# The third pair's q is turned right behind the first run of u, in a linear attention and gated layer kernel

## The chip, the cores and the metric

The kernel runs on one core of a Trainium2 chip. The metric is the time on the device in microseconds (us). Before the change it was 1086.03 us, the median of three runs (1085.31 to 1089.51). The profiled execution, from which all views of the kernel before are taken, has a span of 1088.1 us from its first to its last instruction.

In the text, TensorE (PE in the profile) is the matrix engine, VectorE (DVE) and ScalarE (ACT) are the engines for elementwise work, GpSimd (POOL) forms differences of weights, and SyncE (SP) issues nearly all transfers. Loading the stationary operand of a matmul is an instruction of its own and has its own row, PEld.

## What is computed

Attention without a softmax, an RMS norm per head, and then a gated feed-forward layer:

```python
# q, k, v: batch 8, heads 8, sequence 576, head size 64, all float32
kv = np.einsum('bhsd,bhse->bhde', k, v)
out = np.einsum('bhsd,bhde->bhse', q, kv)          # u in the kernel
rms = np.sqrt(np.mean(out * out, axis=-1, keepdims=True) + 1e-06)
attn = out / rms * g_norm

# x: 4608 tokens of 512 (all heads of one place side by side)
gate = 1.0 / (1.0 + np.exp(-(x @ w_gate)))          # 512 -> 1536
val = x @ w_val                                     # 512 -> 1536
y = gate * val @ w_out                              # 1536 -> 512
```

The three weight matrices are stored as doubles, and the kernel converts them to float32 itself at its start.

## The kernel before

**Two streams of work.** The 4608 tokens are cut into nine chunks of 512 (`G`). The feed-forward layer goes over chunks 0 to 8, and the attention over batches 0 to 7 of 576 tokens. Batches 0 and 1 are computed at the start by an order of tokens written out by hand, together with chunk 0 and the conversion of the weights. From then on, while chunk c (1 to 6) is in the feed-forward layer, the attention of batch c + 1 (2 to 7) is woven into it. This is the part that the change touches; the text calls batches 3 to 7 *later batches*. Chunks 7 and 8 have no attention beside them.

**A chunk of the feed-forward layer.** The chunk is computed by a Strassen-like scheme with seven products in place of eight. The first layer (`first_layer_fast`, line 682) has six blocks. In each, seven steps are taken for two columns of blocks in turn: one product for the first, one for the second (line 692, four matmuls in the source and eight records in the trace), followed by the VectorE or ScalarE instruction that takes the result out of the accumulator bank: a copy (L700), sigmoids (L710, L724), additions (L706, L714, L719, L723, L728). At the end of a block come the two multiplications by the gate (L731) and four sums for the second layer (L761 to L764), all on VectorE. The second layer (`second_layer_fast`, line 766) has 14 products of six matmuls each (line 778); its evacuations are L785 to L808.

**Slots.** The attention of the next batch is a queue of small steps, `fill`. Each call of `slot()` takes one step from the queue and emits it at that place of the program. The first layer calls it after each of the seven steps of a block, so 42 times in a chunk; the second layer calls it after every third matmul, so 28 times. Thus a step's place in the queue is its place in every engine's order of work. [...]`spread` puts the queue together: in the first layer, a step on VectorE is only given slots 2 to 5 of a block (1 to 5 in chunk 1), and empty steps are put in ahead of it until such a slot comes.

**The steps of a batch** come from `feed(b)` (line 341), which handles the four pairs of heads of the batch:

- `turn(n, e)` (line 366): q of pair n, head e, is turned from rows to columns by a VectorE transpose (L369), 96 partitions x 384. There are two turns per pair. The turned q goes to `qTs`, which has room for two pairs (pair n uses half n % 2). Behind the second turn of pair n, `load_q(n + 1)` asks for the q of the next pair (L100, 288 KB). The tile for q has one buffer, so this transfer waits for the second turn to have read it.
- `kv_mm` (L353, L359): k times v of all four pairs on TensorE, and `kv_copies` (L364), eight copies to `kvq` on VectorE.
- `two_pairs(n0)` (line 374), called for the first two pairs and for the last two. It returns nine steps: `u_mm` (L393, 72 small matmuls in the source and 144 records, the first pair's half and then the second's), the square on ScalarE (L399), two sums on VectorE (L402), the root on ScalarE (L405, with a load of another activation table ahead of it), a reciprocal and two norms on VectorE (L409, L411), and two steps that turn the result back (L418, two transposes each) and send it by DMA into the next chunk's x (L428).

At the end of the queue, the sums over the next chunk's x are put in (`x_sums`, L669 to L672), which need those transfers. The accumulator tile of u has one buffer (tag `at`), which `u_mm` of the last two pairs takes over from the first two.

**The order around the change**, in slots of the chunk from 0, for a later batch: turns of the first pair 2 and 3; kv matmuls 8; copies 9 to 19; turns of the second pair 23 and 24; u of the first two pairs 25; square 26; sums 30 and 31; root 32; norms 33 and 37; x turns 38 and 39; turns of the third pair 40 and 42; turns of the fourth pair 44 and 45; u of the last two pairs 46 and the other steps behind it, the last x turn at 54; sums over x asked for at 59. Slot 42 is the first of the second layer.

Of the kernel before, what the change touches and what calls it, by code (L numbers as in the profile page):

```python
# [20 lines left out]
def kernel(  # L21
# [223 lines left out]
    def chunk(c):  # L245
        if c not in xT:
            xT[c] = sb.tile([P, NMT, G], FP32, tag="xT", name="xT", bufs=3)
        return xT[c]
# [90 lines left out]
    PE, DVE, ACT = range(3)  # L339

    def feed(b):

        early = b == 2
        d = {}

        def kv_mm():
            mains, rest = kv_late[b]
            d["kv"] = ps = at_ps()
            for n in range(NHP):
                for j in range(NK4):  # L350
                    for e in range(2):
                        c = slice(NK4 * HD * e + HD * j, NK4 * HD * e + HD * j + HD)
                        nc.tensor.matmul(ps[HD * e:HD * e + HD, n, 0:HD], mains[n, "k"][:, c], mains[n, "v"][:, c],  # L353
                                         start=(j == 0), stop=False)
            for i in range(NHP // 2):
                for r in range(2):
                    for e in range(2):
                        n, rs, c = NHP // 2 * r + i, slice(PH * r, PH * r + PH), HD * (2 * i + e)
                        nc.tensor.matmul(ps[HD * e:HD * e + HD, n, 0:HD], rest[rs, c:c + HD],  # L359
                                         rest[rs, GH + c:GH + c + HD], start=False, stop=True)  # L360

        def kv_copies(i, rs):
            for r in rs:
                nc.vector.tensor_copy(out=kvq[QB * r:QB * r + QB, :, i], in_=d["kv"][QB * i:QB * i + QB, :, 0:HD])  # L364

        def turn(n, e):

            w_ = NJ * HD
            nc.vector.transpose(qTs[0:NP, n % 2, w_ * e:w_ * e + w_],  # L369
                                pairs[n]["q"][:, e].rearrange("p (j i c) -> p i j c", i=NC, c=QB))  # L370
            if e == 1:
                load_q(n + 1)

        def two_pairs(n0):


            d = {}
            ms = sb.tile([P, NQ, NJ], FP32, tag="ms2", name="ms2", bufs=1)
            sq = sqs[:, 0:2 * S].rearrange("p (r c) -> p r c", r=NQ)
            units = [slice(NJ // 2 * i, NJ // 2 * (i + 1)) for i in range(2)]  # L380

            def by_head(t):
                return t.rearrange("p r (n d) -> p r n d", d=HD)

            def u_mm():
                d["u"] = u = at_ps()[:, 0:NQ, 0:2 * QC]
                for which in range(2):
                    for g in range(JH):
                        for i in range(NC):
                            for r in range(NQ):  # L390
                                for e in range(2):
                                    c, o = NJ * HD * e + QC * i + PH * g, HD * (JH * which + g)
                                    nc.tensor.matmul(u[HD * e:HD * e + HD, r, o:o + HD],  # L393
                                                     qTs[QB * r:QB * r + QB, (n0 + which) % 2, c:c + PH],
                                                     kvq[QB * r:QB * r + QB, (n0 + which) % NHP, NC * e + i],
                                                     start=(i == 0), stop=(i == NC - 1))

            def u_square():
                nc.scalar.activation(out=sq, in_=d["u"], func=AF.Square)  # L399

            def u_sum(i):
                nc.vector.tensor_reduce(out=ms[:, :, units[i]], in_=by_head(sq)[:, :, units[i]], axis=AX.X, op=ALU.add)  # L402

            def u_root():
                nc.scalar.activation(out=ms, in_=ms, func=AF.Sqrt, bias=eps, scale=1.0 / HD)  # L405

            def u_norm(i):
                if i == 0:
                    nc.vector.reciprocal(ms, ms)  # L409
                m_ = ms[:, :, units[i]]  # L410
                nc.vector.tensor_tensor(out=by_head(sq)[:, :, units[i]], in0=by_head(d["u"])[:, :, units[i]],  # L411
                                        in1=m_.unsqueeze(3).to_broadcast([P, NQ, NJ // 2, HD]), op=ALU.mult)

            def x_turn(i):


                for which in range(2):
                    nc.vector.transpose(xTs[:, i, which],  # L418
                                        sq.rearrange("p r (w g i c) -> p w i r g c", w=2, g=JH, i=NC)[:, which, i])
                m = n0 % NHP  # L420
                for j in range(2):
                    for e in range(2):
                        p0, p1 = HD * e + QB * j, HD * e + QB * i
                        s0 = 0
                        while s0 < S // 2:
                            c, o = divmod(S * b + S // 2 * j + s0, G)
                            n_ = min(G - o, S // 2 - s0)
                            nc.sync.dma_start(out=chunk(c)[p1:p1 + QB, m:m + 2, o:o + n_],  # L428
                                              in_=xTs[p0:p0 + QB, i, :, s0:s0 + n_])
                            s0 += n_  # L430

            return ([(PE, u_mm), (ACT, u_square), (DVE, lambda: u_sum(0)), (DVE, lambda: u_sum(1)), (ACT, u_root),
                     (DVE, lambda: u_norm(0)), (DVE, lambda: u_norm(1))] +
                    [(DVE, lambda i=i: x_turn(i)) for i in range(NC)])

        def turns_of(n):
            return [(DVE, lambda n=n, e=e: turn(n, e)) for e in range(2)]

        n0 = NHP * b
        steps = turns_of(n0)  # L440

        if b > 2:
            steps += [(PE, idle)] * 4
        steps.append((PE, kv_mm))
        for i in range(2 * NC):
            for rs in ((0, 1), (2,)):
                steps.append((DVE, lambda i=i, rs=rs: kv_copies(i, rs)))
        steps += turns_of(n0 + 1) + two_pairs(n0) + turns_of(n0 + 2) + [(PE, idle)] + turns_of(n0 + 3)
        return steps + two_pairs(n0 + 2) + [(PE, idle)] * 4

    def idle():
        pass
# [61 lines left out]
    def at_ps():  # L514
        return psum.tile([P, 4, 512], FP32, tag="at", name="at")
# [35 lines left out]
    def plain(c, f, ps):  # L551

        blk = Plain(c, f, ps)
        for at in range(2 * NMT):
            blk.mm(*divmod(at, NMT))
            if at in (0, 2) and late:
# [8 lines left out]
    steps = {"KV": KV, "KVO": KV_OUT, "Q": Q, "QO": Q_OUT, "U": U, "SQ": U_SQUARE, "SUM": U_SUM, "ROOT": U_ROOT,  # L565
             "NORM": U_NORM, "X": X, "XO": X_OUT}
# [283 lines left out]
    for c in range(1, NG):  # L850
        if c + 1 < B:
            steps = feed(c + 1)
            if c == 1:

                i = 4
                while w2_sums:
                    steps.insert(i, (DVE, w2_sums.popleft()))
                    i += 3
            spread(steps, (1, 2, 3, 4, 5) if c == 1 else (2, 3, 4, 5))
        first_layer_fast(c)  # L860
        sums_of(c + 1)
        second_layer_fast(c)
        flush()
# [30 lines left out]
```

## Time and profile before

| | before |
|---|---|
| time, median of 3 | 1086.03 us (1085.31 to 1089.51) |
| span of the profiled execution | 1088.1 us, mean granted TensorE clock 0.994 |
| TensorE matmul / weight load busy | 1074.0 us (99%) / 888.0 us (82%) |
| VectorE / ScalarE / GpSimd busy | 637.7 us (59%) / 242.6 us (22%) / 291.3 us (27%) |
| L393, weight loads of u | 1728, busy 21.6 us, 9.5 us idle ahead of them |
| L369, turns of q | 48, busy 26.4 us, 17.3 us idle ahead of them, waiting for q |
| L669, first sum over x | 8, busy 5.5 us, 13.7 us idle ahead of them, waiting for x |

How to read the profile: the page gives busy time per engine and the chain of work that ended last. A list of groups gives, per line and operation, the busy time, the mean time of one, and how long its engine sat idle just before it and what ended that. The chain of waits says who waited for whom, with the total in us, the number of times and the longest. The order of time (timeline) has one line for instructions of a kind that follow each other, with the start, the time to the last one's end, the engine and line, the operation, what is written and read, and their number; in square brackets stands an idle time before it and what ended it. "issue" is time in which the engine waited for nothing that the profile shows. Busy times of matmuls are modelled at their ends; the starts of the weight loads are the firmer measure of when TensorE goes on.

The chunks can be told apart by the first weight load of L692 in each: chunk 2 runs from 275.17 us, chunk 3 from 393.78, chunk 4 from 510.44, chunk 5 from 628.97, chunk 6 from 745.49, chunk 7 from 862.17 and chunk 8 from 970.95.

### The profile page before, as it was taken

What the parts mean: (1) busy time and instruction counts of PE and PEld (TensorE: products, weight loads), DVE (VectorE), ACT (ScalarE), POOL (GpSimd) and SP (SyncE); (2) the same over time, 40 slices, a digit from 0 to 9 for tenths busy, and PEclk for the clock granted to TensorE, in tenths of its full rate; (3) what the DMA queues carried; (4) which work ended last, traced back from release to release, by engine and by line L of the source; (5) the groups of instructions that cost most, each with busy time, mean ns of one, the idle gap of its engine ahead of it and who ended that gap; (6) DMA issues with size and microseconds to landing.
All of it is one profiled execution on the core that took longest, in us unless ns stands there. A gap on an engine that the chain in (4) does not pass through costs nothing.

```text
span 1088.1 us, 18239 instructions
## 1 busy us (share of the span) xinstructions
PE 1074.0 (99%) x7226; PEld 888.0 (82%) x7226; DVE 637.7 (59%) x1261; ACT 242.6 (22%) x473; POOL 291.3 (27%) x390
## 2 busy tenths in 40 slices
PE   9999999999999999999999999999999999999997
PEld 8544448888888888888888888888888888888886
DVE  4897747784477447662767347744766266516631
ACT  4654321221113111311122111311131112001200
POOL 0000024440254024420444025402442055205500
PEclk9999999999999999999999999999999999999998
DMA  9944710012400140013201130024001200010001
GB/s 255 251 155 155 241 39 12 12 25 62 118 12 11 51 130 12 13 45 78 81 12 40 47 118 12 11 57 137 1 12 37 56 3 1 1 37 3 1 1 39
DMA packets 69108, 64.89 MB, mean 60 GB/s; under 512 B 23712, under 2 KB 63008, under 8 KB 69024
## 3 DMA queue, kind: packets, MB, share of 16 engines
q1 hardware_dynamic: 68768, 63.69, 21.1%
q8 instruction: 58, 0.95, 0.4%
q14 instruction: 26, 0.21, 0.1%
q10 hardware_dynamic: 256, 0.03, 0.1%
HBM read 47.19 MB, written 9.44 MB: 52 GB/s over the span
## 4 chain that ended last, share of the span: by engine, by line
PE 93%; DVE 2%; DMA 2%; SPq 1%; issue 1%; ACT 0%; POOL 0%; DVEq 0%; POOLq 0%
PE mm L692 52%; PE mm L778 24%; PE mm L539 7%; PE mm L636 4%; PE at L393 2%; DMA q<-in_q_dram 1%; PE at L353 1%; SPq L428 1%; PE mm L617 1%; DMA xT<-xTs 1%; PE at L539 1%; PE two L261 1%; DVE gv L731 1%; PE two L291 1%; DVE qTs L369 0%
## 5 line engine op out<-in xcount | busy, mean ns | idle before, releaser
L679 POOL TENSOR_TENSOR tw<-gv 128x256 f32<-128x256 f32 x192 | 139.6, 738 | 741.7 <-PE mm L692 589.9
L692 PE MATMUL mm<-xT,tw 128*128 128x256 f32 x768 | 182.0, 380 | 0.0
L692 PE MATMUL mm<-xT,gv 128*128 128x256 f32 x768 | 181.9, 380 | 0.0
L692 PE MATMUL mm<-sx,tw 128*128 128x256 f32 x768 | 181.5, 379 | 0.0
L692 PEld LDWEIGHTS mm<-xT,gv 128*128 128x128 f32 x768 | 145.5, 190 | 20.4 <-issue 0.5
L692 PEld LDWEIGHTS mm<-sx,tw 128*128 128x128 f32 x768 | 145.8, 190 | 19.9
L692 PEld LDWEIGHTS mm<-xT,tw 128*128 128x128 f32 x768 | 145.4, 190 | 19.9
L679 POOL TENSOR_TENSOR tw<-gv,tw 128x256 f32<-128x256 f32 x192 | 157.0, 839 | 0.0
L731 DVE TENSOR_TENSOR gv<-gv,sg 128x512 f32<-128x512 f32 x96 | 93.9, 1017 | 0.0
L778 PE MATMUL mm<-w,gv 128*128 128x256 f32 x384 | 91.8, 388 | 0.0
L692 PE MATMUL mm<-sx,gv 128*128 128x256 f32 x384 | 90.7, 379 | 0.0
L778 PE MATMUL mm<-t2w,gv 128*128 128x256 f32 x384 | 89.3, 383 | 0.0
L724 ACT ACTIVATE sg<-sg 128x256 f32<-128x256 f32 x96 | 39.7, 417 | 222.3 <-DVE sg L723 222.1
L778 PE MATMUL mm<-w,s 128*128 128x256 f32 (+1 forms) x408 | 88.5, 367 | 0.0
L714 DVE TENSOR_TENSOR gv<-mm,sg 128x256 f32<-128x256 f32 x96 | 40.8, 425 | 75.9 <-PE mm L692 75.7
L778 PEld LDWEIGHTS mm<-t2w,gv 128*128 128x128 f32 x384 | 73.9, 193 | 10.7 <-DVE sg L794 0.3
L778 PEld LDWEIGHTS mm<-w,gv 128*128 128x128 f32 x384 | 73.8, 193 | 10.5
L778 PEld LDWEIGHTS mm<-w,s 128*128 128x128 f32 x408 | 74.0, 190 | 9.4
L692 PEld LDWEIGHTS mm<-sx,gv 128*128 128x128 f32 x384 | 73.0, 190 | 9.9
L539 PE MATMUL mm<-xT,gv 128*128 128x512 f32 x176 | 77.4, 594 | 0.0
L700 ACT COPY sg<-mm 128x256 f32<-128x256 f32 x96 | 35.8, 372 | 165.1 <-PE mm L692 164.6
L710 ACT ACTIVATE sg<-mm 128x256 f32<-128x256 f32 x96 | 36.9, 384 | 131.6 <-PE mm L692 131.6
(96 smaller groups left out, 1000.9 us busy)
## 6 DMA issues: line engine op xcount, KB each, us to landing
q<-in_q_dram SPq DMA_DIRECT2D x24, 288.0 KB
st<-in_moe_w_gate_dram SPq DMA_DIRECT2D x12, 512.0 KB
st<-in_moe_w_val_dram SPq DMA_DIRECT2D x12, 512.0 KB
st<-in_moe_w_out_dram SPq DMA_DIRECT2D x12, 512.0 KB
kv<-in_k_dram SPq DMA_DIRECT2D x24, 256.0 KB
kv<-in_v_dram SPq DMA_DIRECT2D x24, 256.0 KB
out_dram<-sg SPq DMA_DIRECT2D x23, 192.0 KB
xT<-xTs SPq DMA_DIRECT2D x48, 72.0 KB
```

The lines of the kernel that those rows point to most:

```text
L261: nc.tensor.matmul(ps[HD * e:HD * e + HD, 0, 0:HD], pairs[n]["k"][:, e, js], pairs[n]["v"][:, e, js], start=(j == 0), stop=(j == NJ - 1))
L393: nc.tensor.matmul(u[HD * e:HD * e + HD, r, o:o + HD], qTs[QB * r:QB * r + QB, (n0 + which) % 2, c:c + PH], kvq[QB * r:QB * r + QB, (n0 + ...
L539: nc.tensor.matmul(self.ps[i], w[("wg", "wv")[i], self.f][:, m, :], xT[self.c][:, m, :], start=(m == 0), stop=(m == NMT - 1), skip_group_c ...
L636: nc.tensor.matmul(ps[t], gv[0, f][:, P * t:P * t + P], w["wo", f], start=(f == 0), stop=(f == NFT - 1), skip_group_check=True)
L679: nc.gpsimd.tensor_tensor(out=tw[f, i], in0=b[in0], in1=b[in1] if isinstance(in1, tuple) else tw[f, in1], op=ALU.subtract)
L692: nc.tensor.matmul(ps, wt[:, m, :], xs[:, m, :], start=(new and m == 0), stop=(m == NK - 1), skip_group_check=True)
L700: nc.scalar.copy(out=d["sg"][:, h2], in_=pa)
L710: nc.scalar.activation(out=d["sg"][:, h1], in_=d["pa"], func=AF.Sigmoid)
L714: tt(out=d["h"][:, h2], in0=d["pb"], in1=d["sg"][:, h2], op=ALU.add)
L724: nc.scalar.activation(out=d["sg"][:, h2], in_=d["sg"][:, h2], func=AF.Sigmoid)
L731: tt(out=d["h"], in0=d["h"], in1=d["sg"], op=ALU.mult)
L778: nc.tensor.matmul(ps, hs(f), ws[:, f, :], start=(new and f == 0), stop=(f == NF2 - 1), skip_group_check=True)
```

## The change

Only the list at the end of `feed` is changed: the order of steps and the empty steps. No instruction is added, removed or changed in shape.

```diff
-        steps += turns_of(n0 + 1) + two_pairs(n0) + turns_of(n0 + 2) + [(PE, idle)] + turns_of(n0 + 3)
-        return steps + two_pairs(n0 + 2) + [(PE, idle)] * 4
+
+        u, *rest = two_pairs(n0)
+        steps += turns_of(n0 + 1) + [u] + rest[:1] + [(PE, idle)] * (3 if b > 2 else 0) + turns_of(n0 + 2) + rest[1:]
+        return steps + [(PE, idle)] + turns_of(n0 + 3) + two_pairs(n0 + 2) + [(PE, idle)] * 5
```

`u` is the step with the u matmuls of the first two pairs and `rest[:1]` their square. The turns of the third pair now follow these, with three empty slots between in a later batch, and all other steps of the first two pairs come behind them. As the third pair's second turn asks for the fourth pair's q, this request comes earlier too. Its purpose is that q of the fourth pair has landed when its turn comes.

In slots of a later batch, after the change: u of the first two pairs 25 and square 26, as before; turns of the third pair 30 and 31; sums 32 and 33; root 34; norms 37 and 38; x turns 39 and 40; turns of the fourth pair 42 and 43; u of the last two pairs 44, the last x turn 52; sums over x asked for at 58. For batch 2, in chunk 1, where twelve sums of the second layer's weights lie between the steps, the third pair's turns go from slots 43 and 44 to 29 and 31, the sums, root, norms and x turns of the first two pairs come three to five slots later, and the fourth pair's turns (47 and 49) and its u (50) stay.

## The prediction

> **What bounds the kernel now.** I began with the page: busy time by engine, then the chain that ended last.
>
> ```profile
> PE 1074.0 (99%) x7226; PEld 888.0 (82%) x7226; DVE 637.7 (59%) x1261; ACT 242.6 (22%) x473; POOL 291.3 (27%) x390
> ...
> PE 93%; DVE 2%; DMA 2%; SPq 1%; issue 1%; ACT 0%; POOL 0%; DVEq 0%; POOLq 0%
> ```
>
> TensorE is the bound nearly everywhere. The change adds and removes no instruction, so it can only win back time in which TensorE stands still. Next I read the chain of waits: first all of it, then TensorE's weight loads alone between 270 and 1080 us, which hold chunks 2 to 8.
>
> ```profile
> DVE qTs L369 <- DMA q<-in_q_dram: 17.3, 6, 3.1
> ```
>
> ```profile
> PEld at L393 <- DVE qTs L369: 5.6, 10, 1.0
> ...
> PEld mm L778 <- DVE sg L794: 0.3, 1, 0.3
> ```
>
> VectorE waits 17.3 us for q in six turns (one in each feed, about 2.9 us). TensorE sees only a part of that: its u matmuls wait for the turned q. Ten waits in five batches means two per batch, and nothing else of size. So the prize is not 17.3 us. To size it, the weight loads of one batch in order of time (chunk 3, which feeds batch 4; columns: start us, length us, instructions):
>
> ```profile
> 441.58 1.66 PEld L393 LDWEIGHTS at<-kvq,qTs 32*64 32x64 f32 x144 [0.33 <-issue]
> 443.31 1.59 PEld L692 LDWEIGHTS mm<-xT,tw 128*128 128x128 f32 x8
> ...
> 470.83 2.56 PEld L778 LDWEIGHTS mm<-w,gv 128*128 128x128 f32 x12
> 473.42 2.56 PEld L778 LDWEIGHTS mm<-t2w,s 128*128 128x128 f32 x12
> 476.01 1.27 PEld L778 LDWEIGHTS mm<-w,gv 128*128 128x128 f32 x6
> 477.61 0.91 PEld L393 LDWEIGHTS at<-kvq,qTs 32*64 32x64 f32 x72 [0.33 <-issue]
> 479.34 0.19 PEld L393 LDWEIGHTS at<-kvq,qTs 32*64 32x64 f32 x2 [0.82 <-DVE qTs L369]
> 479.80 0.90 PEld L393 LDWEIGHTS at<-kvq,qTs 32*64 32x64 f32 x70 [0.27 <-DVE qTs L369]
> 480.77 1.16 PEld L778 LDWEIGHTS mm<-w,gv 128*128 128x128 f32 x6
> ```
>
> The first run of u (call it uA) takes 443.31 - 441.58 = 1.73 us, unhindered. The second (uB) takes 480.77 - 477.61 = 3.16 us: its half for the third pair runs, then it stands until both turns of the fourth pair are there. Read in the same way, uB takes 3.21, 3.16, 3.33, 3.02 and 3.17 us in chunks 2 to 6 and 1.73 in chunk 1. **The loss is 1.48 + 1.43 + 1.60 + 1.29 + 1.44 = 7.24 us**, all in chunks 2 to 6: 0.67% of 1086.03. Why VectorE is late shows in its own order of time:
>
> ```profile
> 471.58 2.09 DVE L731 TENSOR_TENSOR gv<-gv,sg 128x512 f32<-128x512 f32 x2
> ...
> 474.85 0.42 DVE L764 TENSOR_TENSOR s<-gv,s 128x256 f32<-128x256 f32 x1
> 475.18 0.57 DVE L369 STREAM_TRANSPOSE qTs<-q 96x384 f32<-96x384 f32 x1
> 478.72 1.03 DVE L369 STREAM_TRANSPOSE qTs<-q 96x384 f32<-96x384 f32 x2 [2.97 <-DMA q<-in_q_dram]
> ```
>
> There is one q buffer, so the fourth pair's load can be asked for only when the third pair's second turn ends (475.75). It lands 3 us later, and the two turns end at 479.75. The second layer began at 470.83, behind an end of block and four sums which VectorE does first.
>
> [...]Here it is asked for and awaited at once: 2.97 us. [...]L788, queued behind the late turns, starts at 479.68. [...]Two of the five late uBs are followed by that:
>
> ```profile
> 359.00:362.20 3.20, 2.33 (x145) 2.00 (x144) 1.34 (x3) 0.00 (x0) 0.00 (x0) 1.00 0.13 40
> 362.20:365.80 3.60, 3.60 (x13) 2.87 (x10) 1.41 (x2) 1.81 (x3) 0.00 (x0) 0.53 0.28 86
> ```
>
> (Columns: stage, its length, PE, PEld, DVE, ACT, POOL, granted clock, DMA share, GB/s.) Chunk 4 shows the same, 0.54. [...]The trace has the 1283 ns (L405), but no drain: the root at 484.11 follows its load of 482.81 + 1.28 by 0.02 us.
>
> **The change, part by part.** I count slots from 0: 42 in the first layer (seven per block, about 1.73 us each: 8 loads of 0.2155), then 28 in the second (6 loads, 1.29 us).
>
> *The third pair's turns* go from slots 40 and 42 to 30 and 31, so q of the fourth is asked for at 31 and turned at 42: some 11 x 1.73 = 19 us, against the 3 us it needs. The wait of 2.9 us goes. *q of the third pair* keeps its asking slot (24) but is now turned at 30, six slots (10 us) later. Its load was issued at 440.90, so it should be there by 444 or so; old block 4 reached the corresponding VectorE place (slot 30) at 450.92. No wait. The three idle slots keep the turn, which overwrites what uA reads, over 7 us behind uA. Cost 0.
>
> *The sums, root and norms of the first two pairs* slip by two or three slots. Block 4 on VectorE held two sums (0.74 each), reciprocal and norm (0.26 + 0.76) = 2.50 us; now two turns (0.56 each) and two sums = 2.60. Block 5 held norm, two x turns (0.83 each) and a q turn = 2.97; now reciprocal, two norms and two x turns = 3.43. The gaps of 0.25 to 0.70 us in which VectorE waited for TensorE in block 5 take this; the last (0.44 us ahead of the second L728 at 471.24) stays, so L731 still starts at 471.58. ScalarE: the root moves behind the block's last sigmoid (ends 458.31); table 1.28 and root 0.31 end at 459.9, ahead of the copy at 460.07. The sigmoid table then loads behind the copies (461.59 to 462.87), ahead of the sigmoid at 463.47. Cost 0, with 0.2 us to spare.
>
> *Batch 2 (chunk 1)* loses nothing today. Two x turns (four transposes, 1.54 us) take the place of two q turns (1.03) ahead of L788, which then ends at 243.88 + 0.5 = 244.4; the product that overwrites its bank begins at 244.97. Cost 0, little to spare.
>
> *The fourth pair's turns and uB* are the one thing that must be sized. In chunk 3 the turns start when the sums end, 475.18 (q is there), and end at 475.18 + 1.03 = 476.21. uB moves from slot 46 to 44, twelve loads earlier: first load at 470.83 + 18 x 0.2155 + 0.33 = 475.04. Its first half takes 0.91, to 475.95; then it needs the second turn, seen at 476.26 (0.05 later, as at 479.80). From there 0.97 us as now (480.77 - 479.80): next product at 477.23. uB so takes 2.19 us, **0.46 more than 1.73: the early uB still outruns VectorE by a little**. Gain per batch 1.45 - 0.46 = 0.99; five batches **4.9 us**.
>
> *Behind uB* everything comes two slots earlier. The reciprocal waits for a root ending at about 483.5 and lies before L794, which slips by 0.4 us; its bank is overwritten 1.8 us later. The x transfers are issued some 4.7 us earlier, while the next chunk's sums come one slot earlier, so their wait (13.7 us over five chunks, L669) mostly goes, and the 0.3 us it once cost at L794: **0.3 us**.
>
> Sum: 4.9 + 0.3 = 5.2, and 1086.03 - 5.2 = **1080.8 us** (-0.48%).
>
> **Rivals.** *R1, the wait only changes place:* uB comes two slots sooner and VectorE, with 0.5 us more in block 5, reaches the last turns late. Each 0.1 us there costs 0.1 per batch; 0.6 us late makes the loss 1.06 per batch, the gain 0.4 x 5 = 2: 1084. For it: 0.46 us is left already. Against: the 0.44 us gap ahead of the last L728. *R2, slower:* the root with its tables falls in front of the copies that free TensorE's banks. A full table and root (1.6 us) per batch would cost 8 us, less 4.9: 1089. For it: 0.2 us of margin. Against: that margin comes from measured starts in an undisturbed chunk. *R3, more:* the half-clock stretches come from the late uB and go with it. One costs 31.56 - 29.68 = 1.9 us (chunk 2 against chunk 3, from uB to the chunk's end), 0.2 of it the wait above. Runs of 1085.31 to 1089.51 fit none to two; if the median holds one, 1.7 more: 1079.1. If uB is not held up at all: 1078.5. For it: the shorter uB, 2.19 + 0.33 = 2.5 us, is less than the kv matmuls' 2.7, after which no chunk slows.
>
> **How the numbers follow.** Forecast 0.60, R3 0.15, R1 0.17, R2 0.08. The range runs from all of the loss regained (1078.6) to just past R1 (1084.3); R2 and the tails lie outside. Half a per cent is 1080.6, beside the forecast: just over half of its 0.60 falls beyond it, with R3 0.47 faster; the rest with R1 0.45 same; 0.08 slower.
>
> **What would show it.** VectorE's wait for q should fall from 17.3 us to near 0; uB in chunks 2 to 6 should start 3.9 us plus the issue gap behind the second layer's first load and take about 2.2 us; no half clock after it; L700 and L710 no later than now. I am wrong if uB still takes 3 us, if q of the third pair is waited for at slot 30, or if block 5 has new gaps on TensorE.

## The result and the profile after

The changed kernel takes 1080.81 us (median of four runs, 1080.35 to 1081.11), against 1085.95 us for the kernel before (the three runs named above and one more). The ratio is 0.9946, 95% interval 0.9924 to 0.9967. The forecast was 1080.8.

The page of the changed kernel, its busy times and its chain. SyncE's queue and the transfers have all but left the chain:

```profile
PE 1068.8 (99%) x7226; PEld 884.9 (82%) x7226; DVE 636.8 (59%) x1261; ACT 242.5 (22%) x473; POOL 291.3 (27%) x390
...
PE 96%; DVE 2%; issue 0%; DMA 0%; ACT 0%; SPq 0%; POOL 0%; DVEq 0%; POOLq 0%
```

In the whole chain of waits, VectorE's wait for q (17.3 us before) is no longer listed. The wait of the first sum over x (L671 now, L669 before: 13.7 us) is still there. Of TensorE's weight loads between 270 and 1080 us, one wait for the turns is left:

```profile
DVE sx L671 <- DMA xT<-xTs: 7.6, 5, 2.5
```

```profile
PEld at L393 <- DVE qTs L369: 1.3, 5, 0.3
```

Chunk 3 again, the weight loads and then VectorE, in order of time (start, length, instructions). The second layer's line is now L780:

```profile
467.50 2.56 PEld L780 LDWEIGHTS mm<-w,gv 128*128 128x128 f32 x12
470.09 1.27 PEld L780 LDWEIGHTS mm<-t2w,s 128*128 128x128 f32 x6
471.69 0.97 PEld L393 LDWEIGHTS at<-kvq,qTs 32*64 32x64 f32 x74 [0.33 <-issue]
472.93 0.90 PEld L393 LDWEIGHTS at<-kvq,qTs 32*64 32x64 f32 x70 [0.27 <-DVE qTs L369]
473.90 1.16 PEld L780 LDWEIGHTS mm<-t2w,s 128*128 128x128 f32 x6
```

```profile
471.52 0.42 DVE L766 TENSOR_TENSOR s<-gv,s 128x256 f32<-128x256 f32 x1
471.85 1.03 DVE L369 STREAM_TRANSPOSE qTs<-q 96x384 f32<-96x384 f32 x2
475.57 0.42 DVE L790 TENSOR_TENSOR sg<-mm,sg 128x256 f32<-128x256 f32 x1 [2.69 <-PE mm L780]
```

The turns now run right behind the last sum, without a wait for q. uB starts 471.69 - 467.50 = 4.19 us into the second layer (3.86 of loads and the gap of 0.33) and lasts 473.90 - 471.69 = 2.21 us. It does so in each of chunks 2 to 6, where it took 3.02 to 3.33 before. The five gains are 1.00, 0.95, 1.12, 0.81 and 0.96, together **4.84 us**.

The profiled spans differ by more, 1088.1 - 1079.2 = 8.9 us. Most of what uB does not account for is the granted clock: the kernel before had two stretches of 3.41 us at half clock (granted clock 0.50, behind uB in chunks 2 and 4), and the changed one has none before its last weight load ends. Each cost about half its length: the 18 loads of L778 behind uB took 5.47 us in chunk 2 and 5.46 in chunk 4, against 3.78 in chunk 3. Half of both stretches is 3.41 us. The 3.4 us behind uB in chunk 3 (columns as in the prediction; the clock is the 1.00):

```profile
473.90:477.30 3.40, 3.40 (x19) 3.01 (x17) 1.73 (x3) 1.13 (x1) 0.00 (x0) 1.00 0.39 110
```

To compare profiles without their starts, I use the **stretch from the first weight load of chunk 1's second layer to the end of the last load**: 843.11 us before (236.99 to 1080.10) and 834.75 after (236.49 to 1071.24). The difference is 8.36: 4.84 from uB, 3.41 from the half clock, and 0.1 net of small terms.

### The profile page after: what moved, and what is told of

It is laid out like the page before. It is cut to its first block, busy times and chain, and to the rows that moved or that the text cites. A ratio compares the mean times of both kernels' runs of the same rounds, so it can differ in the third digit from the quotient of the medians.

```text
span 1079.2 us, 18246 instructions
## 1 busy us (share of the span) xinstructions
PE 1068.8 (99%) x7226; PEld 884.9 (82%) x7226; DVE 636.8 (59%) x1261; ACT 242.5 (22%) x473; POOL 291.3 (27%) x390
## 4 chain that ended last, share of the span: by engine, by line
PE 96%; DVE 2%; issue 0%; DMA 0%; ACT 0%; SPq 0%; POOL 0%; DVEq 0%; POOLq 0%
PE mm L694 53%; PE mm L780 25%; PE mm L541 7%; PE mm L638 4%; PE at L393 2%; PE at L353 1%; PE mm L619 1%; PE at L541 1%; DVE gv L733 1%; PE two L261 1%; PE two L291 1%; PE two L318 0%; DVE qTs L369 0%; PE two L272 0%; DMA xT<-xTs 0%
## 5 line engine op out<-in xcount | busy, mean ns | idle before, releaser
L780 PE MATMUL mm<-w,s 128*128 128x256 f32 (+1 forms) x408 | 88.6, 367 | 0.0
L780 PE MATMUL mm<-t2w,gv 128*128 128x256 f32 x384 | 88.1, 379 | 0.0
L780 PE MATMUL mm<-w,gv 128*128 128x256 f32 x384 | 88.1, 379 | 0.0
L780 PEld LDWEIGHTS mm<-w,s 128*128 128x128 f32 x408 | 74.0, 190 | 9.4
L780 PEld LDWEIGHTS mm<-w,gv 128*128 128x128 f32 x384 | 73.0, 190 | 9.9
L780 PEld LDWEIGHTS mm<-t2w,gv 128*128 128x128 f32 x384 | 72.9, 190 | 9.9
```

Source lines behind the costliest of these rows:

```text
L780: nc.tensor.matmul(ps, hs(f), ws[:, f, :], start=(new and f == 0), stop=(f == NF2 - 1), skip_group_check=True)
```

## The experiments

The theory: what costs is TensorE's hold in uB (the time in which its weight loads stand for a turn), which ends when VectorE has turned the fourth pair's q, and that turn waits for a load asked for too late. The rivals: the place of uB and of what follows it makes the gain; VectorE's wait itself costs; or another resource takes over.

### e1: the load alone, in the old order

```diff
-            t = sb.tile([NP, 2, NJ * HD], FP32, tag="q", name="q", bufs=1)
+            t = sb.tile([NP, 2, NJ * HD], FP32, tag="q", name="q", bufs=2)
...
-            for i in (n + 4,) if n + 4 < NE else (NE,) if n == NE - 1 else ():
+            for i in (n + 4,) if n + 4 < NE else (NE, NE + 1) if n == NE - 1 else ():
...
-                load_q(n + 1)
+                load_q(n + 2)
```

> The order of the kernel before, with a second q buffer, so that each pair's q is asked for two pairs ahead. My theory (the loss is the hold of the second run of u behind a late q): q of the fourth pair is there when its turn comes, the three turns end about 1.6 us behind the sums, 0.9 us before TensorE reaches the second run at slot 46, so that this run takes 1.73 us in every chunk. Gain 7.2 us on the kernel before: 1078.7 us. Rival (what counts is that the second run and all behind it come two slots sooner): nothing moves, 1086. Rival (a later resource takes over, about half is given back): 1082.

Measured: 1078.62 us (1078.39 to 1079.31), ratio 0.9924 (0.9912 to 0.9937). The weight loads of chunk 3, then VectorE:

```profile
472.13 1.27 PEld L778 LDWEIGHTS mm<-w,gv 128*128 128x128 f32 x6
473.73 1.66 PEld L393 LDWEIGHTS at<-kvq,qTs 32*64 32x64 f32 x144 [0.33 <-issue]
475.46 1.16 PEld L778 LDWEIGHTS mm<-w,gv 128*128 128x128 f32 x6
```

```profile
470.96 0.42 DVE L764 TENSOR_TENSOR s<-gv,s 128x256 f32<-128x256 f32 x1
471.30 1.49 DVE L369 STREAM_TRANSPOSE qTs<-q 96x384 f32<-96x384 f32 x3
```

uB is one unbroken line of 144 loads and takes 1.73 us in all six chunks. Three turns in a row end at 472.79, 0.94 us before uB starts. The steps stand where they stood in the kernel before, so the place of uB is not needed for the gain: an early load is enough. It wins more than the change, because the old place of uB, two slots later, leaves VectorE its time.

### e2: the changed kernel with uB one slot later

```diff
-        return steps + [(PE, idle)] + turns_of(n0 + 3) + two_pairs(n0 + 2) + [(PE, idle)] * 5
+        return steps + [(PE, idle)] + turns_of(n0 + 3) + [(PE, idle)] + two_pairs(n0 + 2) + [(PE, idle)] * 4
```

> The changed kernel, with one empty slot between the fourth pair's turns and the second run of u. My theory: in the changed kernel that run takes 2.21 us since it comes 0.5 us too early for VectorE; six weight loads (1.29 us) later it is not held, and takes 1.73. Gain 5 x 0.48 = 2.4 us on the changed kernel: 1078.4 us. Rival (the small hold covers another wait, such as the banks or the issue gap): 1080.8, with a new wait elsewhere on TensorE.

Measured: 1079.79 us (1078.92 to 1080.74), ratio 0.9933 (0.9921 to 0.9945), 1.4 us above the expectation.

```profile
474.42 1.69 PEld L393 LDWEIGHTS at<-kvq,qTs 32*64 32x64 f32 x144 [0.33 <-PE mm L780]
476.18 2.46 PEld L780 LDWEIGHTS mm<-w,gv 128*128 128x128 f32 x12
```

uB takes 1.76 us here (1.75 to 1.81 in chunks 2 to 6), so the hold is gone. The stretch defined above takes 832.66 us, 2.09 less than in the changed kernel, near the 2.4 expected. In the profile the time that is missing went at the start: the second layer of chunk 1 begins at 238.25 us in place of 236.49. There a transfer of v is on the chain from 9.13 to 18.01 us; TensorE, which works through most of it, waits 1.12 us for that transfer and takes the matmuls that need it at 18.14 in place of 16.44. The start of the program is the same in both kernels. No new wait stands in the feed.

### e3: the changed order with the request left late

```diff
-            if e == 1:
+            if e == 1 and n % NHP != 2:
                 load_q(n + 1)
...
-        return steps + [(PE, idle)] + turns_of(n0 + 3) + two_pairs(n0 + 2) + [(PE, idle)] * 5
+        return steps + [(PE, lambda: load_q(n0 + 3))] + turns_of(n0 + 3) + two_pairs(n0 + 2) + [(PE, idle)] * 5
```

> The changed kernel's order, but q of the fourth pair is asked for behind the first two pairs' x transfers and not behind the third pair's turn. My theory: SyncE issues those transfers until about 6 us into the second layer, q lands 3 us later and the turns take 1 us: the second run of u is held by about 5.2 us in chunks 2 to 6 in place of 0.5, and by as much in chunk 1. Without half clock 1104 to 1109 us; if a hold of this length brings half clock (1.7 us each) every time, up to 1119. Rival (the place of the turns and of u makes the gain, not the request): 1081.

Measured: 1130.05 us (two runs, 1129.23 and 1130.87), ratio 1.0396 (1.0375 to 1.0418). The direction is clear, and the size was missed. In chunk 3, SyncE, VectorE, and TensorE's loads:

```profile
482.27 7.79 SPq L428 DMA_DIRECT2D xT<-xTs  x12
490.11 5.09 SPq L100 DMA_DIRECT2D q<-in_q_dram  x2
```

```profile
493.82 1.03 DVE L369 STREAM_TRANSPOSE qTs<-q 96x384 f32<-96x384 f32 x2 [5.27 <-DMA q<-in_q_dram]
```

```profile
488.30 0.92 PEld L393 LDWEIGHTS at<-kvq,qTs 32*64 32x64 f32 x72 [0.33 <-issue]
494.45 0.28 PEld L393 LDWEIGHTS at<-kvq,qTs 32*64 32x64 f32 x2 [5.24 <-DVE qTs L369]
494.91 1.38 PEld L393 LDWEIGHTS at<-kvq,qTs 32*64 32x64 f32 x70 [0.17 <-DVE qTs L369]
```

The request went out where I placed it, behind the twelve x transfers, but q took 3.7 us (490.11 to 493.82) in place of 3.0, with those transfers under way. Then TensorE came back at half clock (granted clock 0.52 from 492.4 to 499.0 us): the last 70 loads took 1.38 us in place of 0.90. uB takes 8.1 us here, 8.1 to 9.2 over the six chunks. All six bring half clock, five times for two stretches of 3.41 us and once for three, 44.4 us in all (mean granted clock 0.979, against 0.998 in the changed kernel). Of these, 15.3 us lie inside the holds, where TensorE stands anyway; the other 29.1 are put at half their length, as measured in the kernel before: 14.6 us, an estimate. The loads' waits for the turns come to 35.7 us, against 1.3 in the changed kernel. The two, 34.4 and 14.6, are near the 48.1 us by which the stretch grew (882.87 against 834.75). The expectation had 5.2 us of hold per chunk, where 5.4 to 6.5 came, and had allowed one half-clock stretch each.

So the same order of steps wins 5 us with the early request and loses 43 us without it. The request is what works. Its place here is a little later than in the kernel before (6.0 us into the second layer against 4.9), so e3 does not say what moving uB forward costs by itself; e5 does.

### e4: the old order with uB one slot later

```diff
-        return steps + two_pairs(n0 + 2) + [(PE, idle)] * 4
+        return steps + [(PE, idle)] + two_pairs(n0 + 2) + [(PE, idle)] * 3
```

> The order of the kernel before, with one empty slot ahead of the second run of u and nothing else. Theory that only TensorE's standing counts: VectorE still waits some 17 us for q, but TensorE does 1.29 us of products in the time, and reaches the half that needs the fourth pair just as its turn ends (first load 478.9 + 0.9 = 479.8 against 479.8 in chunk 3): a hold of 0 to 0.15 us, 1078.6 to 1079.5 us, less than the changed kernel. Rival (the wait of VectorE for q is itself what costs, since evacuations stand behind it): little is gained, 1083 to 1086.

Measured: 1080.33 us (1079.22 to 1081.45), ratio 0.9941 (0.9927 to 0.9955). In order of time, VectorE and the weight loads:

```profile
474.96 1.03 DVE L369 STREAM_TRANSPOSE qTs<-q 96x384 f32<-96x384 f32 x2 [2.92 <-DMA q<-in_q_dram]
```

```profile
475.20 1.75 PEld L393 LDWEIGHTS at<-kvq,qTs 32*64 32x64 f32 x144 [0.33 <-issue]
477.02 2.46 PEld L778 LDWEIGHTS mm<-t2w,gv 128*128 128x128 f32 x12
```

VectorE still waits 2.92 us here, 16.9 us in all. TensorE does not feel it: uB takes 1.82 us, and 1.76 to 1.89 over chunks 2 to 6. The rival that VectorE's wait itself costs falls. The stretch takes 832.80 us, 2 us less than in the changed kernel. The six times lie near 1079.3 or near 1081.4. The profiled execution shows no wait of that size in the feed, and no trace shows what separates the two groups.

### e5: the old order with uB one slot sooner

```diff
-        steps += turns_of(n0 + 1) + two_pairs(n0) + turns_of(n0 + 2) + [(PE, idle)] + turns_of(n0 + 3)
-        return steps + two_pairs(n0 + 2) + [(PE, idle)] * 4
+        steps += turns_of(n0 + 1) + two_pairs(n0) + turns_of(n0 + 2) + turns_of(n0 + 3)
+        return steps + two_pairs(n0 + 2) + [(PE, idle)] * 5
```

> The kernel before with its one empty slot between the third and fourth pair's turns taken out, so that the second run of u stands one slot (1.29 us) sooner, while q of the fourth pair is asked for and lands as before. Theory (TensorE's hold is what costs): the hold of 1.45 us grows by 1.29 to 2.7 in chunks 2 to 6, the run of u to 4.5 us, 6.5 us more in all: 1092.5 to 1093 us if the half clock stays as rare as before. Theory of the half clock (a hold that makes the run of u longer than some 3.3 us brings it): a stretch of 3.41 us at half clock behind each of the five, 1.7 us each, so 1098 to 1101. Rival (the hold is measured wrongly, something else made the gain): near 1086.

Measured: 1100.79 us (1099.85 to 1102.88), ratio 1.0115 (1.0101 to 1.0129). The stages of chunk 3, uB and then a part of what follows it (stage, length, PE, PEld, DVE, ACT, POOL, granted clock, DMA share, GB/s):

```profile
478.98:483.39 4.41, 2.34 (x146) 2.00 (x145) 1.34 (x3) 0.00 (x0) 0.00 (x0) 1.00 0.24 73
484.20:487.40 3.20, 3.20 (x9) 2.58 (x8) 1.41 (x2) 0.42 (x1) 0.00 (x0) 0.50 0.11 41
```

uB takes 5.12, 4.41, 4.75, 4.33 and 4.46 us, 7.18 us more in sum than in the kernel before (6.5 expected). Half clock follows all five, with 20.5 us of it in place of 6.8 (mean granted clock 0.990, against 0.994 in the kernel before); at half the length this is another 6.8 us, an estimate. The sum is 14.0; 0.7 of it is counted twice, since half clock sets in at 361.27 us while uB of chunk 2 runs until 362.93. The rest, 13.3, fits the 13.4 us by which the stretch grew (856.55 against 843.11). So an earlier uB without an earlier request is a loss.

### e6: the changed order with two q buffers

The edit is that of e1, made in the changed kernel.

> The changed kernel with a second q buffer and q asked for two pairs ahead. My theory: in the changed kernel the load is no longer what holds TensorE, the 0.48 us per batch that are left are VectorE's turns ending behind the place of u, so nothing changes: 1080.8, second run of u 2.21 us. Rival (the load still plays a part, for instance through the transfers it shares the queue with): up to 2.4 us less, 1078.4.

Measured: 1081.06 us (1080.63 to 1081.19), ratio 0.9931 (0.9917 to 0.9944). uB takes 2.21 us in chunks 2 to 6 and the stretch 834.76 us against 834.75. Once the change is made the load plays no part. What is left is VectorE's two turns behind its sums.

### e7: the root behind the copies

```diff
-        steps += turns_of(n0 + 1) + [u] + rest[:1] + [(PE, idle)] * (3 if b > 2 else 0) + turns_of(n0 + 2) + rest[1:]
+        steps += turns_of(n0 + 1) + [u] + rest[:1] + [(PE, idle)] * (3 if b > 2 else 0) + turns_of(n0 + 2) + rest[1:3] + [(PE, idle)] + rest[3:]
```

> The changed kernel with the root of the first two pairs one slot later, behind the next block's two copies, so that both table loads (2 x 1.28 us) and the root come between those copies and the sigmoids. Theory of the prediction's second rival (tables ahead of ScalarE's evacuations hold TensorE): the first sigmoid starts 1.0 us later, about 1 us per batch is lost, 1086. My theory: the bank that this sigmoid reads is written again only two steps (3.45 us) behind its product, so the delay is taken by that room: no hold, 1080.8, with the sigmoid about 1 us later in the order of time.

Measured: 1081.37 us (1081.05 to 1082.63), ratio 0.9936 (0.9924 to 0.9949). ScalarE in order of time:

```profile
459.17 0.37 ACT L702 COPY sg<-mm 128x256 f32<-128x256 f32 x1 [0.49 <-PE mm L694]
459.56 1.28 ACT L405 ACT_TABLE_LOAD   x1
460.86 0.31 ACT L405 ACTIVATE ms<-ms,eps 128x18 f32<-128x18 f32 x1
461.18 1.28 ACT L712 ACT_TABLE_LOAD   x1
462.48 0.66 ACT L712 ACTIVATE sg<-mm 128x256 f32<-128x256 f32 x2
```

The first sigmoid starts about 0.8 us later in its chunk than in the changed kernel (70.47 us after the chunk's first load in place of 69.69), and TensorE does not notice: the stretch takes 834.83 us against 834.75. The rival of slow tables falls at this size.

## Why the prediction was right

**The prize.** VectorE waited 17.3 us, but the forecast took the 7.24 us that TensorE stood. e4 confirms this reading: it keeps VectorE's wait (16.9 us) and recovers the loss.

**The size.** The forecast had uB at 2.19 us and 0.46 us of hold left; the trace shows 2.21 and 0.48 in every chunk. The gain in uB was put at 4.9 and measured at 4.84. It follows from two sums of time that run from the same point: VectorE's (end of block, sums, two turns) and TensorE's (18 loads, the gap, half of uB). e2 moves the second by one slot and the hold vanishes; e6 speeds up the load and nothing happens. VectorE's turns start 4.35 us into the second layer, as before (475.18 - 470.83 and 471.85 - 467.50), though the gap ahead of the last addition of block 5 (L730 now) did not stay at 0.44 us but shrank to 0.24.

**What costs nothing.** The third pair's q was there at slot 30: no turn waits for q. The table, the root and block 5 took no time of TensorE. The root ends 0.15 us ahead of the next copy, near the 0.2 us that I stated, but that is not the margin that counts: in the program the copied bank is written again two steps later. The bank that the first sigmoid reads has the same room; e7 puts off this sigmoid by 0.8 us, and nothing is lost. No run puts off the copies. In chunk 1 the product behind L788 was not held, as forecast; its uB took 1.78 in place of 1.73, which I had not seen.

**The small terms.** The wait for x was to go mostly; it fell only from 13.7 to 7.6 us. The first sum over x moved one slot ahead, past L790, and now waits there (1.38 us in chunk 3) while VectorE would wait for TensorE anyway (2.75 us of that follow). The hold of 0.3 us at L794 is gone.

**The rivals.** R1 fails: the loss that was left is the one computed. R2 fails: the copies come no later than before (10.75 us ahead of the second layer, against 10.76). R3 was right that the half clock goes with the late uB (two stretches before, none after), but the median did not hold it: the fall of 5.14 us in the medians is 4.84 and the small terms, within the spread of the runs. Only the profiled execution of before, with two such stretches, shows 8.9. In the later sets of runs the kernel before had medians of 1086.65 and 1088.31 us, while e6, the changed kernel's twin, stayed at 1081.06. Half clock in before fits that: the mean granted clock on record is 0.994 to 0.997 in the nine runs behind the 1088.31, and 0.998 or 0.999 in those of e6, where one stretch of 3.41 us lowers the mean by 0.0016 (half of it in 1086 us). Those runs left no trace, so where it lay is not shown. It is partly luck, then, that the four runs of the result had a median without it, and that the forecast met 1080.81 to 0.01 us is chance: the four runs spread over 0.76 us, and the small terms, put at 0.3, came to 0.1 in the traces.

**What would have been better.** One more q buffer in the old order (e1, 1078.62 us) beats both kernels, and one empty slot ahead of uB (e4, 1080.33) does about as much as the whole change.

## What to carry to other kernels

Size a wait on the engine that sets the end: a wait of 17 us on VectorE was worth 7 on TensorE. When two engines meet at a point, compute both arrival times from a common start. Once the load comes early, the later of the two still sets the time, and an instruction that is moved forward with it can use up part of the gain. Before reordering, try the second buffer and the one empty slot.

## What the runs showed of the hardware

Short holds can cost more than their length. In the kernel before, the holds of 1.48 and 1.60 us in chunks 2 and 4 were followed by half clock, and the 18 loads behind them took 1.69 and 1.68 us longer than in chunk 3. With a uB of 1.73 to 2.21 us no half clock followed (after, e1, e2, e4, e6, e7; mean granted clock 0.998 or 0.999). With 3.02 to 3.33 us it followed twice in five, behind the two longest (3.21 and 3.33); with 4.33 to 5.12 us (e5) every time for at least 3.41 us; with 8.1 to 9.2 us (e3) for 6.83 us or more.

The traces' record of the granted clock puts the two stretches of the kernel before at 362.38 and 597.90 us, 0.17 and 0.29 us behind the end of uB, each 3.413 us long. No uB between 2.21 and 3.02 us was measured, and five between 3.02 and 3.33 are too few to say at which length half clock sets in. What decides it is not shown; the small u matmuls were not tried by themselves.
